# First attention pair: scores from split float32r operands of 64 rows, its rotation on VectorE, and zero matmuls ahead of the first data

## The chip, the cores and the metric

One core of a Trainium2 chip. Every time is in microseconds (us) on the device; a kernel's time is the median of its runs. The profile is one further execution, with its own time.

## The reference

Three stages in a row. Attention over 4 batches, 8 heads, 576 positions, head size 64; then two feed-forward blocks on the 2304 resulting rows of 512.

```python
q_rot, k_rot = rotate(q), rotate(k)          # rotary: x1*cos - x2*sin, x1*sin + x2*cos
scores = q_rot @ k_rot.T / sqrt(64)
attn = softmax(scores) @ v                   # -> x, 2304 x 512
h = x @ w_in;  x2 = (h - tanh(h)) @ w_out    # 512 -> 2048 -> 512
out = ((x2 @ w1) * (x2 @ w2)) @ w3 @ w_out2  # 512 -> 1024 -> 512
```

The change touches the attention alone, and there only what is done for the first of its 16 pairs of heads.

## The kernel before

**Pairs and steps.** Two heads of one batch are a pair, and lie on the partitions as 2 x 64 rows (head j in rows 64j to 64j+63). The 576 positions are 512 main ones and 64 tails. A pair has five steps (`steps`, L416): first c = NQ = 4, the tail queries of both heads in one block, then c = 0 to 3, 128 main queries for each head. I call them NQ and c0 to c3.

**One step.** `scores` (L298) writes one PSUM tile "sc" per head (two banks each; NQ has only one tile; there are two "sc" buffers in all), `exps` (L331) reads it on ScalarE, with the maximum that VectorE's reduction L327 found as bias. `norm` divides on GpSimd, `trans` (L359) transposes the result on TensorE three steps later (LAG_T), and `pv` multiplies by v from four steps later.

**The two ways of making scores.** From the second pair on, q and k are split in two float32r parts (hi and the rest), and `prep_q`, `prep_k` and `prep_t` (L219, L241, L264) move them by DMA into tiles of 128 rows (`qs`, `ks`), so that two matmuls of 128 rows and 288 columns give the three products. The first pair doesn't wait for such DMAs: `q_first`, `k_first` and `qt_first` are plain float32 tiles, and its scores are float32 matmuls whose operands are 64 rows of them (the trace shows two PE instructions for each). All four of head 0 come first, then the four of head 1.

**The rotation.** `rope` (L193) makes two products with the sine table on VectorE (L199), one product with the cosine table (L202) and a sum (L204). While `early[0]` is true, that is for the first pair and the first tails, L202 runs on GpSimd and L204 on VectorE.

**The order.** The program text is a list; a scheduler puts each engine's instructions in order, by place in the text and by what is ready in its own reckoning. On the chip each engine takes its list strictly in that order. The head (L467 to L481) is: DMAs for k, its table, tails, q, its table, the second pair, two weights; then rotation of k, `prep_k`, rotation of q and of the tails, `prep_t`, `prep_q`; then the loop over steps (L484), in which `prepare` (L446) makes the next pair ready in steps NQ, c0 and c1.

Of the kernel before, what the change touches and what calls it, by code (L numbers as in the profile page):

```python
# [42 lines left out]
def fused_kernel(tc, q, k, v, w_in, w_out, w1, w2, w3, w_o2, tables, out):  # L43
# [14 lines left out]
    def f32(ap):  # L58
        return ap.bitcast(F32)
# [133 lines left out]
    def rope(t, cos, sin, a):  # L193

        p, n, C = t.shape[0], t.shape[1], t.shape[2]
        a = a.rearrange("p c h d -> p h c d")
        hd = D // 2
        for o, i in ((0, hd), (hd, 0)):
            nc.vector.tensor_tensor(  # L199
                a[:, :, :, o:o + hd], t[:, :, :, i:i + hd],  # L200
                sin[:, :, o:o + hd].unsqueeze(1).to_broadcast([p, n, C, hd]), ALU.mult)
        (nc.gpsimd if early[0] or n > 2 else nc.vector).tensor_tensor(  # L202
            t, t, cos.unsqueeze(1).to_broadcast([p, n, C, D]), ALU.mult)
        (nc.vector if early[0] else nc.gpsimd).tensor_tensor(a, a, t, ALU.add)  # L204
# [12 lines left out]
    qk, first = {}, {}  # L217

    def prep_q(b, hp):  # L219
        a = rot["q", b, hp]  # L220
        ps = psum.tile([128, 512], F32, tag="t", name=f"tq_{b}_{hp}", bufs=4)
        for c in range(NQ):
            nc.tensor.transpose(ps[:, c * 128:(c + 1) * 128],
                                a[:, c, :, :].rearrange("p h d -> p (h d)"), ident)
        if (b, hp) == pairs[0]:
            t = att.tile([128, SM], F32, tag="qs0", name="q_first")
            nc.any.tensor_copy(t, ps)
            first["q"] = t
            return
        qp = slots.tile([128, 2, SM], F32R, tag="s15", name=f"qp_{b}_{hp}")  # L230
        nc.any.tensor_copy(qp[:, 0, :], ps)
        nc.vector.tensor_tensor(qp[:, 1, :], ps, f32(qp[:, 0, :]), ALU.subtract)
        qs = []
        for j in range(2):
            t = att.tile([128, SM], F32R, tag=f"qs{j}", name=f"qs{j}_{b}_{hp}")
            for r in range(2):
                nc.sync.dma_start(f32(t[64 * r:64 * r + 64]), f32(qp[64 * j:64 * j + 64, r, :]))
            qs.append(t)
        qk["q", b, hp] = qs

    def prep_k(b, hp):  # L241
# [9 lines left out]
        if (b, hp) == pairs[0]:  # L251
            t = att.tile([128, ST + S], F32, tag="ks0", name="k_first")
            nc.scalar.copy(t[:, ST:ST + SM], ps)
            first["k"] = t
            return
        kp = att.tile([128, 2, ST + S], F32R, tag="kp", name=f"kp_{b}_{hp}", bufs=1)
        m = slice(ST, ST + SM)
        nc.any.tensor_copy(kp[:, 0, m], ps)
        nc.vector.tensor_tensor(kp[:, 1, m], ps, f32(kp[:, 0, m]), ALU.subtract)
        qk["kp", b, hp] = kp  # L260
# [3 lines left out]
    def prep_t(b, hp):  # L264
# [5 lines left out]
        if (b, hp) == pairs[0]:  # L270
            t = att.tile([128, 128], F32, tag="qs1", name="qt_first")
            nc.gpsimd.memset(t, 0.0)
            first["t"] = t
            for j in range(2):
                p = slice(64 * j, 64 * j + 64)
                nc.vector.tensor_copy(t[p, p], ps[p, 0:64])
            for o in (0, ST + SM):
                nc.vector.tensor_copy(first["k"][:, o:o + 64], ps[:, 64:128])
            return
# [5 lines left out]
        ends = kp.rearrange("p t (n s) -> p t n s", s=ST)[:, :, ::S // ST, :]  # L285
        twice = ps[:, 64:128].unsqueeze(1).to_broadcast([128, 2, ST])
        nc.scalar.copy(ends[:, 0], twice)
        nc.vector.tensor_tensor(ends[:, 1], twice, f32(ends[:, 0]), ALU.subtract)
        for j, t in enumerate(qk["k", b, hp]):
            src = kp[64 * j:64 * j + 64, :, ST:] if j == 0 else kp[64:128, :, 0:S]  # L290
            for r in range(2):
                nc.sync.dma_start(f32(t[64 * r:64 * r + 64]), f32(src))
        qk["qt", b, hp] = qt
# [4 lines left out]
    def scores(i):  # L298
        b, hp, c = steps[i]
        e = att.tile([128, 2, S], F32, tag="e", name=f"e_{i}", bufs=E_BUFS)  # L300
        ss = []
        for j in range(2 if c < NQ else 1):
            s = psum.tile([128, 2, 512], F32, tag="sc", name=f"sc{j}_{i}", bufs=2)
            ss.append(s)
            for n in range(2):
# [3 lines left out]
                q_c = slice(c * 128, (c + 1) * 128)  # L309
                if (b, hp) == pairs[0]:  # L310
                    if c < NQ:
                        p = slice(64 * j, 64 * j + 64)
                        terms = [(first["q"][p, q_c], first["k"][p, keys if j else cols])]
                    else:
                        terms = [(first["t"], first["k"][:, cols])]
                elif c < NQ:
                    qs, ks = qk["q", b, hp], qk["k", b, hp]
                    terms = [(qs[j][:, q_c], ks[j][:, t, keys]) for t in range(2)]
                else:
                    qt, kp = qk["qt", b, hp], qk["kp", b, hp]  # L320
                    terms = [(qt[:, x, :], kp[:, y, cols]) for x, y in ((0, 0), (0, 1), (1, 0))]
                for t, (lhs, rhs) in enumerate(terms):
                    nc.tensor.matmul(s[:, n, 0:HS], lhs, rhs,  # L323
                                     start=t == 0, stop=t == len(terms) - 1)
# [141 lines left out]

    load_pair(*pairs[0], "k")  # L467
# [6 lines left out]
    next_load()  # L474
    rope_pair(*pairs[0], "k")
    prep_k(*pairs[0])
    rope_pair(*pairs[0], "q")
    rope_tail(0)
    prep_t(*pairs[0])
    prep_q(*pairs[0])  # L480
# [377 lines left out]
```

## Time and profile before

| what | us |
|---|---|
| median of 3 runs (lowest, highest) | 1120.63 (1110.46, 1121.62) |
| the profiled execution, its own time | 1120.93 |
| its span, first to last instruction | 1119.1 |
| first pair's scores, first matmul to the second pair's first | 13.5 to 42.1 |
| end of the last pair's exponentials | 321 |

The page gives each engine's busy time, the span in 40 slices, the DMA queues, and the chain that ended last, followed back from the end. A busy PE in it is an engine with a matmul in flight, at whatever clock. The rows on which the prediction rests stand in a section of their own below.

### The profile page before, as it was taken

Reading aid. Unit: us, or ns where it says so; the run is one execution under the profiler, and the core shown is the slowest. Engines: PE = TensorE matmul, PEld = TensorE weight load, DVE = VectorE, ACT = ScalarE, POOL = GpSimd, SP = SyncE. Lnnn points to the kernel's source line nnn. Section 1 sums busy time; section 2 is a strip of 40 time slices with the busy share of each in tenths; the row PEclk is TensorE's granted clock in tenths of the full one; section 3 lists DMA queues with packets and bytes.
Section 4 is the critical chain, followed back from the end, with each engine's and each line's share of the span. In section 5 each row is a group of like instructions: output and inputs, shape, how many; then the busy total and the mean of one; then the engine's idle time right before and its main releaser. Section 6 shows DMA issues by size and latency. Waiting matters only on the chain.

```text
span 1119.1 us, 15718 instructions
## 1 busy us (share of the span) xinstructions
PE 1066.4 (95%) x5598; PEld 856.6 (77%) x5598; DVE 783.2 (70%) x1439; ACT 563.0 (50%) x1195; POOL 394.1 (35%) x379
## 2 busy tenths in 40 slices
PE   6999899999998999999989899999899999999998
PEld 3676777777766788888767588898677888888887
DVE  5799999999959868669999978678985211212121
ACT  2577787777766555456656455555532111111121
POOL 3475686676472302024353320316531202002000
PEclk9999999999999999999999899999999999999999
DMA  5465667665612111012222111232531100101010
GB/s 178 122 174 139 176 157 203 158 173 127 167 38 76 38 57 57 29 36 87 76 73 97 57 48 50 92 114 95 205 124 47 38 1 1 38 1 38 1 38 20
DMA packets 64685, 96.37 MB, mean 86 GB/s; under 512 B 11616, under 2 KB 40288, under 8 KB 64608
## 3 DMA queue, kind: packets, MB, share of 16 engines
q1 hardware_dynamic: 64608, 95.38, 29.6%
q8 instruction: 44, 0.72, 0.3%
q14 instruction: 33, 0.27, 0.1%
HBM read 58.79 MB, written 11.01 MB: 62 GB/s over the span
## 4 chain that ended last, share of the span: by engine, by line
PE 66%; DVE 21%; issue 4%; ACT 4%; DMA 2%; POOL 1%; SPq 0%; DVEq 0%; ACTq 0%; POOLq 0%
PE pw L748 15%; PE x2p L581 11%; PE h L544 10%; PE o L771 8%; PE sc L323 7%; PE pv L408 4%; PE wp L628 4%; PE te L381 3%; DVE nm L327 2%; DVE g_q L562 2%; DVE g L567 2%; DVE g_s L561 1%; DVE g_q L564 1%; DVE g_t L563 1%; ACT e L334 1%
## 5 line engine op out<-in xcount | busy, mean ns | idle before, releaser
L581 PE MATMUL x2p<-g,s_out 128*128 128x512 f32 (+1 forms) x960 | 222.4, 378 | 22.3 <-DVE g L567 11.7
L581 PEld LDWEIGHTS x2p<-g,s_out 128*128 128x128 f32 x960 | 170.7, 193 | 63.1 <-DVE g L567 17.8
L345 POOL TENSOR_SCALAR e<-e,r 128x576 f32<-128x576 f32 x144 | 126.0, 887 | 81.7 <-DVE r L343 52.5
L754 DVE TENSOR_TENSOR ab<-a,pw 128x512 f32<-128x512 f32 (+1 forms) x40 | 25.3, 633 | 174.5 <-PE pw L748 173.9
L334 ACT ACTIVATE e<-sc,nm 128x576 f32<-128x576 f32 x144 | 107.8, 748 | 42.9 <-DVE nm L327 30.4
L327 DVE TENSOR_REDUCE nm<-sc 128x1 f32<-128x576 f32 x144 | 106.1, 747 | 21.4 <-PE sc L323 20.6
L771 PE MATMUL o<-wpt,abs 128*128 128x512 f32 x432 | 105.2, 390 | 0.7 <-DVE abs L757 0.5
L566 ACT CAST g<-g_q 128x512 fp32r<-128x512 f32 (+1 forms) x80 | 46.2, 578 | 106.8 <-DVE g_q L564 106.6
L771 PEld LDWEIGHTS o<-wpt,abs 128*128 128x128 f32 x432 | 80.3, 188 | 18.2 <-DVE abs L757 1.1
L323 PE MATMUL sc<-ks,qs 128*128 128x288 f32 x480 | 90.1, 318 | 3.5 <-ACT e L334 3.1
L323 PEld LDWEIGHTS sc<-ks,qs 128*128 128x128 f32 x480 | 67.9, 188 | 26.0 <-ACT e L334 11.5
L381 PE MATMUL te<-ident,e 128*128 128x128 f32 x576 | 84.9, 280 | 0.6 <-ACT eta L385 0.2
L561 DVE TENSOR_TENSOR g_s<-g_s,h 128x512 f32<-128x512 f32 (+1 forms) x80 | 50.4, 630 | 49.7 <-ACT g_m L560 49.4
L752 ACT COPY a<-pw 128x512 f32<-128x512 f32 (+1 forms) x40 | 21.7, 543 | 114.8 <-PE pw L748 114.8
L557 ACT ACTIVATE g_s<-h 128x512 f32<-128x512 f32 (+1 forms) x80 | 44.0, 550 | 61.2 <-PE h L544 59.8
L381 PEld LDWEIGHTS te<-ident,e 128*128 128x128 f32 x576 | 69.4, 145 | 6.3 <-issue 4.2
L567 DVE TENSOR_TENSOR g<-g_q,g 128x512 fp32r<-128x512 f32 (+1 forms) x80 | 59.0, 738 | 16.2 <-ACT g L566 15.4
L756 ACT CAST abs<-ab 128x512 fp32r<-128x512 f32 (+1 forms) x40 | 23.1, 576 | 84.3 <-DVE ab L754 84.3
L564 DVE COPY_PREDICATED g_q<-g_m,g_t 128x512 f32<-128x512 int32 (+1 forms) x80 | 62.9, 787 | 0.8
L562 DVE SCALAR_TENSOR_TENSOR g_q<-g_q,g_s 128x512 f32<-128x512 f32 (+1 forms) x80 | 61.5, 769 | 0.0
L558 ACT ACTIVATE g_q<-g_s,qb 128x512 f32<-128x512 f32 (+1 forms) x80 | 54.5, 681 | 2.6 <-DVE g L567 2.6
L560 ACT ACTIVATE g_m<-g_s,nt 128x512 f32<-128x512 f32 (+1 forms) x80 | 54.0, 676 | 0.0
(387 smaller groups left out, 2302.0 us busy)
## 6 DMA issues: line engine op xcount, KB each, us to landing
ks<-kp SPq DMA_DIRECT2D x60, 288.0 KB, 5.2
raw_w<-in_moe_w SPq DMA_DIRECT2D x32, 512.0 KB, 3.7
raw_in<-in_moe_w_in SPq DMA_DIRECT2D x16, 512.0 KB, 3.7
raw_out<-in_moe_w_out SPq DMA_DIRECT2D x16, 512.0 KB, 3.5
qs<-qp SPq DMA_DIRECT2D x60, 128.0 KB, 3.5
wp_dram<-wpe SPq DMA_DIRECT2D x24, 256.0 KB, 2.0
k<-in_k SPq DMA_DIRECT2D x16, 256.0 KB, 3.2
q<-in_q SPq DMA_DIRECT2D x16, 256.0 KB, 3.0
```

The source lines that it names most:

```text
L323: nc.tensor.matmul(s[:, n, 0:HS], lhs, rhs, start=t == 0, stop=t == len(terms) - 1)
L327: nc.vector.tensor_reduce(nm[:, j:j + 1], s[:, :, 0:HS], AX.XY, ALU.max, negate=True)
L334: nc.scalar.activation(d["e"][:, j, :].rearrange("p (n s) -> p n s", n=2), d["ss"][j][:, :, 0:HS], AF.Exp, bias=d["nm"][:, j:j + 1], accum ...
L345: nc.gpsimd.tensor_scalar(d["e"][:, j, :], d["e"][:, j, :], r[:, j:j + 1], 1.0, ALU.mult, ALU.mult)
L381: nc.tensor.transpose(ps[:, n * 128:(n + 1) * 128], e[:, o + n * 128:o + (n + 1) * 128], ident)
L544: nc.tensor.matmul(ps[:, 0:w], ws[:, a, kk], x[:, b_, 0:w], start=kc == 0 and t == 0, stop=kc == NK - 1 and t == 2)
L562: nc.vector.scalar_tensor_tensor(qq, qq, QC, s, ALU.add, ALU.mult)
L564: nc.vector.copy_predicated(qq, mk.bitcast(I32), t)
L567: nc.vector.tensor_tensor(g[:, 1, 0:w], qq, f32(g[:, 0, 0:w]), ALU.subtract)
L581: nc.tensor.matmul(x2ps[j][o][:, 0:w], ws[:, a, oo], g[:, b_, 0:w], start=c == 0 and t == 0, stop=c == HF - 1 and t == 2)
L748: nc.tensor.matmul(ps[:, 0:w], ws[:, a, kk], x[:, b_, 0:w], start=kc == 0 and t == 0, stop=kc == NK - 1 and t == 2)
L771: nc.tensor.matmul(outps[j][t], g[:, a, tt], wp[c][:, b_, :], start=c == 0 and i == 0, stop=c == NF2 - 1 and i == 2)
```

## The change

Four edits, all for the first pair:

1. `q_first`, `k_first`, `qt_first` go. `prep_q`, `prep_k` and `prep_t` split into float32r parts as for the other pairs, into slots that are not in use yet, and stop before the DMAs.
2. `scores` of the first pair takes three float32r products (hi by hi, hi by rest, rest by hi) straight from these 64-row tiles, and the matmuls of both heads alternate: head 0, head 1, head 0, and so on.
3. In `rope`, the cosine product of the first pair and the first tails moves from GpSimd to VectorE.
4. A tile of zeros is made, and 20 + 8 + 8 matmuls of 128 rows by 512 columns on it are put ahead of the rotation of k, ahead of that of q, and ahead of `prep_q`. Nothing reads their result.

```diff
-        (nc.gpsimd if early[0] or n > 2 else nc.vector).tensor_tensor(
+        (nc.gpsimd if n > 2 and not early[0] else nc.vector).tensor_tensor(
             t, t, cos.unsqueeze(1).to_broadcast([p, n, C, D]), ALU.mult)
...
+    TERMS = ((0, 0), (0, 1), (1, 0))
...
-        if (b, hp) == pairs[0]:
-            t = att.tile([128, SM], F32, tag="qs0", name="q_first")
-            nc.any.tensor_copy(t, ps)
-            first["q"] = t
-            return
-        qp = slots.tile([128, 2, SM], F32R, tag="s15", name=f"qp_{b}_{hp}")
+        first = (b, hp) == pairs[0]
+        qp = slots.tile([128, 2, SM], F32R, tag="s12" if first else "s15", name=f"qp_{b}_{hp}")
         nc.any.tensor_copy(qp[:, 0, :], ps)
         nc.vector.tensor_tensor(qp[:, 1, :], ps, f32(qp[:, 0, :]), ALU.subtract)
+        qk["qp", b, hp] = qp
+        if first:
+            return
...
         if (b, hp) == pairs[0]:
-            t = att.tile([128, ST + S], F32, tag="ks0", name="k_first")
-            nc.scalar.copy(t[:, ST:ST + SM], ps)
+            kp = [slots.tile([128, ST + S], F32R, tag=f"s{10 + t}", name=f"kp{t}_first")
+                  for t in range(2)]
...
+        nc.any.tensor_copy(kp[0][:, m], ps)
+        nc.vector.tensor_tensor(kp[1][:, m], ps, f32(kp[0][:, m]), ALU.subtract)
...
+                elif i < NQ + 1:
+                    p = slice(64 * j, 64 * j + 64)
+                    terms = [(qk["qp", b, hp][p, x, q_c], kp[y][p, keys if j else cols])
+                             for x, y in TERMS]
...
+                mms += [(n, t, j, t == len(terms) - 1, *ops) for t, ops in enumerate(terms)]
+        if i < NQ + 1:
+            mms.sort(key=lambda m: m[:3])
+        for n, t, j, last, lhs, rhs in mms:
+            nc.tensor.matmul(ss[j][:, n, 0:HS], lhs, rhs, start=t == 0, stop=last)
...
+    idle = slots.tile([128, SM], F32R, tag="s9", name="idle")
+    nc.gpsimd.memset(f32(idle), 0.0)
+    idle_ps = psum.tile([128, 512], F32, tag="t", name="idle_ps", bufs=4)
+
+    def spin(n):
+        for _ in range(n):
+            nc.tensor.matmul(idle_ps, idle[:, 0:128], idle, start=True, stop=True)
...
+    spin(20)
     rope_pair(*pairs[0], "k")
     prep_k(*pairs[0])
+    spin(8)
     rope_pair(*pairs[0], "q")
     rope_tail(0)
     prep_t(*pairs[0])
+    spin(8)
     prep_q(*pairs[0])
     early[0] = False
```

## Rows read from the trace of the kernel before

**Rows 1.** The page: busy time of two engines; the granted clock in 40 slices.
```profile
PE 1066.4 (95%) x5598; PEld 856.6 (77%) x5598; DVE 783.2 (70%) x1439; ACT 563.0 (50%) x1195; POOL 394.1 (35%) x379
PEclk9999999999999999999999899999999999999999
```
**Rows 2.** Windows: stretch, length, busy us of engines (instructions), granted clock, DMA share, GB/s.
```profile
13.50:42.10 28.60, 28.60 (x74) 16.93 (x73) 14.53 (x35) 12.88 (x32) 8.99 (x10) 1.00 0.53 139
44.70:321.00 276.30, 266.43 (x1888) 202.76 (x1886) 262.04 (x606) 207.13 (x534) 178.61 (x181) 1.00 0.62 158
339.30:341.70 2.40, 0.17 (x1) 0.00 (x0) 2.37 (x3) 0.85 (x2) 1.52 (x1) 1.00 0.48 191
341.70:345.10 3.40, 2.99 (x7) 2.41 (x8) 3.33 (x7) 2.65 (x5) 0.00 (x0) 0.50 0.00 0
400.00:420.00 20.00, 20.00 (x93) 16.54 (x92) 11.36 (x19) 10.32 (x18) 0.00 (x0) 1.00 0.20 68
```
**Rows 3.** The chain in order of time: start, us, what; first pair and after.
```profile
13.53 4.14 PE sc L323 x8
...
18.93 2.22 PE sc L323 x4
...
38.45 2.21 PE sc L323 x4
40.67 1.04 PE te L381 x4
...
42.14 1.44 PE sc L323 x6
43.58 1.40 PE te L381 x7
...
47.74 0.73 PE sc L323 x4
...
52.22 0.44 PE te L381 x4
...
57.05 1.87 PE pv L408 x14
...
61.60 0.88 PE sc L323 x6
```
**Rows 4.** Timeline of the head: start, us, engine, line, operation, [idle before].
```profile
0.94 0.31 POOL L184 MEMSET zero<- 128x256 f32 x1
4.59 0.76 DVE L199 TENSOR_TENSOR rak<-k,tab 128x256 f32<-128x256 f32 x2 [2.72 <-DMA tab<-tables]
5.43 1.26 POOL L202 TENSOR_TENSOR k<-k,tab 128x512 f32<-128x512 f32 x1 [3.71 <-DVE rak L199]
6.81 0.76 DVE L199 TENSOR_TENSOR rt<-tqk,tab 128x256 f32<-128x256 f32 x2 [1.46 <-DMA tqk<-in_k]
7.49 0.68 DVE L204 TENSOR_TENSOR rak<-rak,k 128x512 f32<-128x512 f32 x1
8.22 1.11 PE L248 MATMUL tk_first<-ident,rak 128*128 128x128 f32 x4 [8.22 <-DVE rak L204]
12.42 1.12 PE L223 MATMUL tq<-ident,raq 128*128 128x128 f32 x4 [1.37 <-DVE raq L204]
```
**Rows 5.** Timeline inside the first pair, from one score tile to its release.
```profile
17.60 1.11 PE L248 MATMUL tk<-ident,rak 128*128 128x128 f32 x4
19.68 0.69 DVE L259 TENSOR_TENSOR kp<-tk,kp 128x512 fp32r<-128x512 f32 x1 [0.19 <-ACT kp L258]
21.18 0.76 DVE L327 TENSOR_REDUCE nm<-sc 128x1 f32<-128x576 f32 x1 [0.81 <-PE sc L323]
21.97 0.74 ACT L334 ACTIVATE e<-sc,nm 128x576 f32<-128x576 f32 x1 [1.36 <-DVE nm L327]
22.61 0.19 ACT L334 ACTIVATION_READ_ACCUMULATOR e<-sc,nm 128x1 f32 x1
31.76 0.58 ACT L385 COPY eta<-te 128x512 f32<-128x512 f32 x1 [1.63 <-PE te L381]
```
**Rows 6.** Timeline: the second pair's DMA issues, and the first matmuls after a fall.
```profile
29.21 3.83 SPq L237 DMA_DIRECT2D qs<-qp  x4
342.11 2.07 PE L581 MATMUL x2p<-g,s_out 128*128 128x512 f32 x4 [2.65 <-ACT g L566]
343.99 0.63 PE L544 MATMUL h<-xs_(0, 0)_2_4331,s_in 128*128 128x512 f32 x1
```

More of the change, by code (lines that the diff above doesn't have):

```diff
@@ L214, in rope_tail @@
         rot["t", b] = a
-    qk, first = {}, {}
+    qk = {}
+    TERMS = ((0, 0), (0, 1), (1, 0))
     def prep_q(b, hp):
@@ L251, in prep_k @@
         if (b, hp) == pairs[0]:
-            t = att.tile([128, ST + S], F32, tag="ks0", name="k_first")
-            nc.scalar.copy(t[:, ST:ST + SM], ps)
-            first["k"] = t
-            return
[L256 to L260, printed above, removed]
+            kp = [slots.tile([128, ST + S], F32R, tag=f"s{10 + t}", name=f"kp{t}_first")
+                  for t in range(2)]
+        else:
+            kp = att.tile([128, 2, ST + S], F32R, tag="kp", name=f"kp_{b}_{hp}", bufs=1)
+            qk["kp2", b, hp] = kp
+            kp = [kp[:, t, :] for t in range(2)]
+        m = slice(ST, ST + SM)
+        nc.any.tensor_copy(kp[0][:, m], ps)
+        nc.vector.tensor_tensor(kp[1][:, m], ps, f32(kp[0][:, m]), ALU.subtract)
+        qk["kp", b, hp] = kp
+        if (b, hp) == pairs[0]:
+            return
         qk["k", b, hp] = [
@@ L269, in prep_t @@
             ident)
[L270 to L279, printed above, removed]
         kp = qk["kp", b, hp]
@@ L284, in prep_t @@
             nc.vector.tensor_tensor(qt[p, 1, p], ps[p, 0:64], f32(qt[p, 0, p]), ALU.subtract)
[L285 removed]
+        ends = [t.rearrange("p (n s) -> p n s", s=ST)[:, ::S // ST, :] for t in kp]
         twice = ps[:, 64:128].unsqueeze(1).to_broadcast([128, 2, ST])
[L287 to L288 removed]
+        nc.scalar.copy(ends[0], twice)
+        nc.vector.tensor_tensor(ends[1], twice, f32(ends[0]), ALU.subtract)
+        qk["qt", b, hp] = qt
+        if (b, hp) == pairs[0]:
+            return
+        both = qk["kp2", b, hp]
         for j, t in enumerate(qk["k", b, hp]):
[L290 removed]
+            src = both[64 * j:64 * j + 64, :, ST:] if j == 0 else both[64:128, :, 0:S]
             for r in range(2):
                 nc.sync.dma_start(f32(t[64 * r:64 * r + 64]), f32(src))
[L293 removed]
     HS = S // 2
@@ L300, in scores @@
         e = att.tile([128, 2, S], F32, tag="e", name=f"e_{i}", bufs=E_BUFS)
[L301 to L304, printed above, removed]
+        ss = [psum.tile([128, 2, 512], F32, tag="sc", name=f"sc{j}_{i}", bufs=2)
+              for j in range(2 if c < NQ else 1)]
+        kp, q_c = qk["kp", b, hp], slice(c * 128, (c + 1) * 128)
+        mms = []
+        for j in range(len(ss)):
             for n in range(2):
```

18 lines of the change are left out of this document (4 added, 14 removed).

## The prediction, made before the changed kernel was run

> **What bounds the kernel now.** I read the page first: TensorE is busy 95% of the span, VectorE 70%, so what TensorE does sooner should come out at the end [rows 1]. Then the stretches. While the first pair's scores run, 13.5 to 42.1 us, TensorE is busy for all of its 28.60 us with only 74 instructions, VectorE for half; from there to 321 us it does 1888 in 276.3 us, nearly seven a microsecond against 2.6, with VectorE at 262.04 us of it [rows 2]. So the first pair is bound by TensorE alone, and slowly; the fifteen pairs after it are bound by TensorE and VectorE together, at (321 - 42.1) / 15 = 18.6 us a pair. The first takes 28.6.
>
> Why so slowly, the chain tells. Four transposes cost 1.04 us at 40.67 and 0.44 at 52.22; six float32r matmuls of 288 columns cost 1.44 at 42.14 and 0.88 at 61.60 (0.24 and 0.147 each) [rows 3]. The same work takes 1.6 to 2.4 times as long, so I take it that TensorE ran on its lower level, 1.2 GHz, until the seven transposes of 43.58 ended (0.20 each). The clock column says 1.00 there [rows 2]; I trust the durations, and read that column as having no record yet. TensorE's work before 42 us had no rest but was nearly all float32 matmuls of 64 rows and transposes; the rise came behind the first float32r matmuls of 128 rows. Where the column does show a fall, it came after 2.40 us in which TensorE had one instruction [rows 2].
>
> **What the change removes, on TensorE.** In steps c0 to c3, from 13.53 + 4.14 - 2.21 = 15.46 to 42.14, that is 26.68 us, the chain holds eight score tiles at 2.21 each, 17.7 us (three of these pieces are in the rows; in the first, two NQ matmuls stand with the tile), and 9.0 us of transposes [rows 3]. A step is 6.67 us.
>
> **What it adds on TensorE.** Twelve float32r matmuls of 64 rows by 288 columns a step, which no row of before shows. Bounds, on the upper level: 12 at the 0.73 / 4 = 0.18 of the 128-row form give 2.2 us; six pairs at half of the low-clock 0.24 give 0.72. I take that the two heads overlap, as the v product does, whose matmuls take half the array's columns in alternation and come at 1.87 / 14 = 0.134, where full ones of that length would need twice as much by their columns [rows 3]: 12 x 0.09 = 1.1 us. On the lower level twice that, 2.2; without overlap 12 x 0.24 = 2.9. Three quarters of the score time go. The Trainium skill says as much: by "TensorE: Matmul & The Clock Gate" (What overlaps and what doesn't), matmuls in different row groups start some 4 ns apart; the sum by it would be the low end, 0.72 a step and 1.5 us less over the pair than mine. No run so far shows it for rows.
>
> **What is late next.** The alternation has a price. Before, head 0's tile needs only its own buffer, while the other is still read. Now the second matmul of a step belongs to head 1, so a step can't go on until both exponentials of the last have read their tiles. Step by step [rows 5]: scores end, reduction 21.18 to its exponential at 21.97, 0.83 with the hand-over; that exponential 0.64 to its accumulator read, 0.10 on to the next; a copy of a transposed tile between the two, 0.48 (31.76; without it 0); head 1's exponential 0.74; 0.05 to TensorE. Sum 2.84 us, without the copy 2.36. Head 1's reduction is done meanwhile. So a step is at least 1.1 + 2.84 = 3.9 us, whatever else TensorE does in between: its transposes, 9.0 / 4 / 2 = 1.1 us a step, fit into the wait. VectorE stands behind other pieces of up to 0.69 us when a tile comes; half a piece, 0.35, makes 4.3.
>
> The Trainium skill warns here: "Tiling speeds up TensorE but not PSUM evacuation" (TensorEngine Tiling (Array Packing), PSUM Bottleneck). This trace agrees, with 2.84 us of evacuation behind 1.1 us of matmul.
>
> TensorE now works only 1.1 + 1.1 of 4.3 us a step. That is above the stretch that preceded the fall (next to nothing in 2.40 us), below the 96% of the later pairs [rows 2], so I expect the clock to fall in part of the pair: two of the four steps with 2.2 in place of 1.1. The four steps: 4 x 4.3 + 2 x 1.1 = 19.4 us. Saved 26.7 - 19.4 = **7.3 us**. VectorE's 14.53 us of work in the old stretch, plus nothing new in c0 to c3, fit into 19.4; ScalarE's 12.88 too.
>
> **After the pair.** From 42.14 to about 44.7 the second pair ran on the lower level: 6 matmuls at 0.24 against 0.147 to 0.18, and five transposes at 0.20 against 0.11, **0.9 us** saved if the clock is up by then.
>
> **The head.** The cosine product of k took 1.26 us on GpSimd, and VectorE did the tails meanwhile; on VectorE it is one piece like L204's 0.68, so k's rotation ends at about 5.35 + 0.68 + 0.68 = 6.7 in place of 8.2 [rows 4]. VectorE has then three such products more (2.0 us) and the parts of k, q and the tails (two at 0.69, three small ones about 0.7), less the small copies that go; starting at 4.6 that ends near 12, and it had gaps of 1.46 us and more. But TensorE's list decides. The zeros are ready at about 0.94 + 0.31 + 0.62 (a memset twice as long) and a little, 2.3. A matmul of 512 columns costs (343.99 - 342.11) / 4 = 0.47 on the lower level [rows 6], 20 / 93 = 0.215 on the upper [rows 2]. If the clock rises half-way, at 7, ten cost 4.7 and ten 2.15: the first twenty end at 9.2, the k transposes come at 9.2 (before 8.22), 0.44 long, then eight zeros 1.7, the tail's transpose, eight zeros 1.7, q's transposes 0.44: 13.5, with VectorE done. q's parts need a copy 0.58 and a subtraction 0.69, so c0 starts at 14.9 with NQ's 1.1 us behind that cover. Against 15.46 that is **0.5 us** saved. If the list takes all 36 zeros first (the trace shows that it does move ready work forward: `tk` of the second pair runs at 17.60 between the score tiles of one step [rows 5]), they end at 12.5, q's transposes at 13.5, and c0 is the same within 0.7. Without a rise, see rival three. The head's bounds are +1.3 and -7.4.
>
> **DMAs.** None is added. The second pair's c0 needs `qs`, issued from 29.21 to 33.04 on SP's queue [rows 6]. It needed them at 47.7; now at about 15 + 19.4 + 4 = 38. Their issue moves forward with the splits of the second pair, so they cost nothing; if they don't move at all, there are still some 5 us less a landing of about 3.
>
> **Sum.** 7.3 + 0.9 + 0.5 = 8.7 us. The profiled execution took 1120.93, 1.8 us more than its span and 0.3 above the median, so 1120.9 - 8.7 = **1112 us**. All later stages should only move: after 42 us TensorE is at 96% and what feeds it has its place in the same lists. One of the three runs was 10 us below the others. No trace of it is here; a run in which the clock rose at the first scores would gain about as much, and then a part of this gain has already been in it.
>
> **Rivals.**
> *One, faster (chance 0.2):* the clock stays up and VectorE isn't in the way: 4 x 3.9 = 15.6, saved 11.1 + 0.9 + 0.5, **1108.5**; with the low end of the matmuls 1107. For it: VectorE has half its time free in this stretch. Against: TensorE idles half of it.
> *Two, the matmuls don't overlap or the clock is down for the whole pair (0.2):* 2.2 to 2.9 us a step, the middle 2.6 + 2.84 + 0.35 = 5.8, four 23.2, saved 3.5, nothing behind it, head 0.5: **1117**. For it: 64-row matmuls never raised the clock before. Against: the column halves overlap.
> *Three, slower (0.1):* multiplying zeros doesn't raise the clock, and all 36 stand ahead of the k transposes: 36 x 0.47 + 2.3 = 19.2; then transposes 0.8, k's parts 1.4, NQ 1.44, so c0 starts at 22.9, 7.4 us late, and the slow steps of rival two give back only 3.5: **1125**. It decides as soon as the zeros end more than 7 us after the k rotation is ready. For it: nothing in this trace shows what zeros do to the clock. Against: instructions of that form hold the upper level for whole stages [rows 2].
> *My forecast* has 0.5, and its own range is 1109 to 1115.
>
> **The numbers.** Rivals one to two span 1107 to 1117, three adds 1125; leaving out half of three and the edge of one, the range is 1106.5 to 1119.5. A measurement here can tell about 1% from no change, that is below 1109.4 or above 1131.8. Below: most of rival one (0.17) and a part of my case (0.14), 0.31. Above: the far end of three, 0.04. Within: 0.65.
>
> **What would show it.** Zeros on TensorE from about 2.3 us, their spacing going from 0.47 to 0.215 before 10; first `tk` transposes at 8.5 to 10 and 0.44 long; c0's scores at about 15; twelve matmuls in 1.1 (to 2.2); each step's scores waiting on ScalarE's second exponential, steps of 4 to 5 us; the second pair's first scores near 34 in place of 42.1; the attention's end near 312. It is wrong if the second pair starts as early as that but the end of the attention doesn't move (VectorE would then be the bound), or if the zeros keep their 0.47 spacing.

## The result, and the profile after

The changed kernel took **1124.3 us** (median of 20 runs, 1122.01 to 1128.36). The kernel before, run beside it 20 times, took 1120.6 (1109.81 to 1124.20). The ratio on record, which is taken over all runs and is not that of the medians (1.0033), is 1.0075 with an interval of 1.0049 to 1.0100: slightly slower, where 1112 was forecast. The profiled execution took 1127.65 (two of the 20 runs took longer) with a span of 1125.8; one further execution that was profiled later took 1121.18. Two single runs took over twice as long as all others, 3628.57 (br_pin) and 2644.13 (before, beside b_mask and nm_pin), and are left out of the medians, ranges and ratios below.

The median of before hides two groups: 9 of its 20 runs lay between 1109.8 and 1111.9, the other 11 between 1120.6 and 1124.2, and nothing between. The trace of [rows 1] is of the upper group. The changed kernel has one group only.

The page of after: busy time of the engines, then the granted clock in 40 slices. The first slice has the clock at 0.6, where [rows 1] has a 9.

```profile
PE 1070.5 (95%) x5652; PEld 867.3 (77%) x5652; DVE 789.2 (70%) x1445; ACT 563.6 (50%) x1196; POOL 385.9 (34%) x376
PEclk9699999998999999999999999999999999999999
```

Windows of after (columns as in [rows 2]). The second row answers to the first there; its clock is 0.66. The third is the stretch between the fall of the clock and its next rise: TensorE busy for nearly all of it, at the lower level (0.50), with 92 instructions in 23.89 us.

```profile
8.20:13.50 5.30, 5.30 (x16) 4.13 (x15) 3.85 (x8) 1.20 (x2) 0.00 (x0) 1.00 0.79 272
13.50:42.10 28.60, 27.22 (x113) 21.31 (x112) 19.67 (x42) 13.38 (x35) 8.91 (x9) 0.66 0.54 136
22.69:46.58 23.89, 23.75 (x92) 19.80 (x92) 14.33 (x36) 13.00 (x33) 7.75 (x10) 0.50 0.40 90
44.70:321.00 276.30, 262.13 (x1850) 201.52 (x1849) 256.51 (x597) 202.74 (x522) 170.27 (x177) 0.98 0.62 156
```

Timeline of after, TensorE (answers to [rows 4, 5]): the head, one step of the first pair, the hand-over to the second pair, and a stall much later.

```profile
6.95 0.66 PE L249 MATMUL tk_first<-ident,rak 128*128 128x128 f32 x2 [6.95 <-DVE rak L204]
7.26 7.23 PE L471 MATMUL idle_ps<-idle 128*128 128x512 f32 x20
14.33 0.38 PE L249 MATMUL tk_first<-ident,rak 128*128 128x128 f32 x2
14.47 2.09 PE L471 MATMUL idle_ps<-idle 128*128 128x512 f32 x8
...
18.36 0.60 PE L225 MATMUL tq<-ident,raq 128*128 128x128 f32 x4
...
21.94 0.53 PE L321 MATMUL sc<-kp_first,qtd 128*128 128x288 f32 x2 [0.85 <-DVE kp_first L282]
...
22.73 4.85 PE L321 MATMUL sc<-kp_first,qp 64*128 64x288 f32 x16
...
31.74 1.80 PE L321 MATMUL sc<-kp_first,qp 64*128 64x288 f32 x6
33.47 1.11 PE L378 MATMUL te<-ident,e 128*128 128x128 f32 x4
34.52 1.81 PE L321 MATMUL sc<-kp_first,qp 64*128 64x288 f32 x6
...
43.00 1.79 PE L321 MATMUL sc<-kp,qtd 128*128 128x288 f32 x6
...
240.25 0.80 PE L321 MATMUL sc<-ks,qs 128*128 128x288 f32 x4 [1.57 <-ACT e L331]
```

The scheduler put the first 20 zeros *between* the second and the third of the four k transposes. They waited for k until 6.95, as the transposes before them did, and then held up the rest of k until 14.33. They did raise the clock, at 12.45 (their spacing goes from 0.43 to 0.23). VectorE's timeline shows what the late k let in:

```profile
12.43 0.43 DVE L115 TENSOR_SCALAR z_in<-z_in 128x512 f32<-128x512 f32 x1 [1.13 <-ACT z_in L113]
...
15.43 0.68 DVE L261 TENSOR_TENSOR kp_first<-tk_first,kp_first 128x512 fp32r<-128x512 f32 x1
...
17.36 1.65 DVE L120 SCALAR_TENSOR_TENSOR z_in<-raw_in,z_in 128x512 int32<-128x512 int32 x1
...
19.77 1.79 DVE L118 SCALAR_TENSOR_TENSOR z_out<-raw_out,z_out 128x512 int32<-128x512 int32 x1
21.59 0.29 DVE L282 TENSOR_TENSOR kp_first<-tt,kp_first 128x128 fp32r<-128x128 f32 x1
```

Conversions of weights (`z_in`, `z_out`) that the kernel needs hundreds of microseconds later stand ahead of k's last part (21.59), for which TensorE waits 0.85 us before 21.94.

Where the 6.7 us between the two profiled executions lie (times of before from [rows 3] and its timeline):

| from, to | before | after | change |
|---|---|---|---|
| start to c0's scores | 15.46 | 22.73 | +7.3 |
| c0's scores to the second pair's first scores | 26.68 | 20.27 | -6.4 |
| these to the second pair's first exponential (45.5; 45.7) | 3.4 | 2.7 | -0.7 |
| that to the end of the last pair's exponentials (320.9; 327.2) | 275.4 | 281.5 | +6.1 |
| that to the end of the span | 798.2 | 798.6 | +0.4 |

(Two of c0's twelve matmuls had gone ahead at 20.56; the table counts from the other ten, at 22.73.) So the pair's saving came, the head ate it, and the fifteen pairs behind it, which were only to move, lost six more. In the later execution of after that stretch was 277.7, +2.3.

### The profile page after: what moved, and what is told of

Read it like the earlier page. It is cut to its first block, busy times and chain, and to the rows that moved or that the text cites. A ratio compares the mean times of both kernels' runs of the same rounds, so it can differ in the third digit from the quotient of the medians.

```text
span 1125.8 us, 15823 instructions
## 1 busy us (share of the span) xinstructions
PE 1070.5 (95%) x5652; PEld 867.3 (77%) x5652; DVE 789.2 (70%) x1445; ACT 563.6 (50%) x1196; POOL 385.9 (34%) x376
## 4 chain that ended last, share of the span: by engine, by line
PE 60%; DVE 26%; ACT 5%; issue 5%; DMA 2%; POOL 2%; DVEq 0%; SPq 0%; ACTq 0%; POOLq 0%
PE pw L757 15%; PE x2p L590 9%; PE h L553 8%; PE o L780 8%; PE sc L321 6%; PE pv L405 4%; PE wp L637 3%; PE te L378 3%; DVE nm L324 3%; DVE g_q L571 2%; DVE g L576 2%; DVE g_q L573 2%; DVE g_s L570 2%; DVE g_t L572 2%; ACT e L331 2%
## 5 line engine op out<-in xcount | busy, mean ns | idle before, releaser
L342 POOL TENSOR_SCALAR e<-e,r 128x576 f32<-128x576 f32 x144 | 120.5, 849 | 85.9 <-DVE r L340 48.6
L324 DVE TENSOR_REDUCE nm<-sc 128x1 f32<-128x576 f32 x144 | 106.5, 749 | 19.9 <-PE sc L321 18.7
L780 PEld LDWEIGHTS o<-wpt,abs 128*128 128x128 f32 x432 | 80.4, 188 | 17.8 <-DVE abs L766 1.0
L573 DVE COPY_PREDICATED g_q<-g_m,g_t 128x512 f32<-128x512 int32 (+1 forms) x80 | 65.4, 818 | 0.8
```

The costliest lines, as they stand in the source:

```text
L324: nc.vector.tensor_reduce(nm[:, j:j + 1], s[:, :, 0:HS], AX.XY, ALU.max, negate=True)
L342: nc.gpsimd.tensor_scalar(d["e"][:, j, :], d["e"][:, j, :], r[:, j:j + 1], 1.0, ALU.mult, ALU.mult)
L573: nc.vector.copy_predicated(qq, mk.bitcast(I32), t)
L780: nc.tensor.matmul(outps[j][t], g[:, a, tt], wp[c][:, b_, :], start=c == 0 and i == 0, stop=c == NF2 - 1 and i == 2)
```

## The experiments

Medians (of ten runs, b_mask of four, n_pin2 of twelve, nm_pin2 of eleven, br_pin of nine), each with the ratio to the kernel before on the same chip; the first two rows are single executions. "Body" is the stretch of 275.4 above, from the second pair's first exponential to the end of the last; the times in the last three columns are of the one execution that was profiled.

| kernel | us (lowest, highest) | ratio, interval | clock up, down, up | second pair's first exponential | body |
|---|---|---|---|---|---|
| before (again, three executions) | 1123.2; 1121.16; 1110.87 | | 45.6; 45.4; 16.3 | 45.5; 46.3; 33.3 | 276.8; 275.5; 276.3 |
| after (again) | 1121.18 | | 10.2, 23.8, 44.3 | 44.7 | 277.7 |
| nospin | 1117.78 (1116.14, 1119.71) | 1.0015 [0.9981, 1.0050] | 35.75 | 41.9 | 275.9 |
| dvezero | 1121.88 (1120.27, 1123.62) | 1.0056 [1.0019, 1.0093] | 7.55, 17.79, 41.7 | 40.7 | 281.2 |
| b_spin | 1124.02 (1122.45, 1125.93) | 1.0080 [1.0042, 1.0118] | 8.4, 18.6, 49.3 | 47.3 | 278.0 |
| alt | 1122.7 (1121.99, 1124.23) | 1.0076 [1.0042, 1.0110] | 40.7 | 42.9 | 279.2 |
| dvz_alt | 1122.88 (1121.31, 1125.83) | 1.0064 [1.0030, 1.0097] | 7.56, 17.80, 41.7 | 42.8 | 280.7 |
| rot | 1122.41 (1121.05, 1127.07) | 1.0062 [1.0027, 1.0097] | 15.0, 18.45, 42.3 | 42.1 | 278.1 |
| b_pin | 1124.3 (1113.39, 1128.73) | 1.0073 [1.0026, 1.0120] | 44.5 | 46.0 | 281.0 |
| br_pin | 1115.15 (1113.34, 1122.88) | 1.0008 [0.9965, 1.0052] | 10.35, 17.2, 41.1 | 41.1 | 281.0 |
| n_pin | 1116.46 (1113.57, 1118.36) | 1.0015 [0.9974, 1.0055] | 12.9, 16.3, 33.4 | 39.8 | 275.2 |
| n_mask | 1112.15 (1110.52, 1114.12) | 0.9950 [0.9917, 0.9983] | 22.65 | 35.9 | 276.5 |
| b_mask | 1117.89 (1116.36, 1120.47) | 1.0075 [1.0055, 1.0096] | 16.3 | 33.4 | 281.2 |
| nm_pin | 1110.44 (1108.27, 1113.44) | 0.9971 [0.9937, 1.0006] | 10.3 | 33.4 | 276.3 |
| n_pin2 | 1117.29 (1114.39, 1119.94) | 1.0013 [0.9979, 1.0047] | 10.9, 17.7, 34.8 | 39.2 | 274.9 |
| nm_pin2 | 1111.20 (1108.82, 1112.66) | 0.9954 [0.9922, 0.9987] | 15.4 | 34.1 | 276.2 |

The ratios hang on how the runs of before split into their two groups beside each kernel; medians in microseconds compare better between rows, to some 1.5 us, by which the middle of each group of before differs between the chips.

**1. The place of the zeros.** *nospin* is after without its zero matmuls (nothing reads their result). *dvezero* changes one word of after. *b_spin* is before with the zeros alone.

```diff
-        for _ in range(n):
+        for _ in range(0):
```

```diff
-    nc.gpsimd.memset(f32(idle), 0.0)
+    nc.vector.memset(f32(idle), 0.0)
```

> The changed kernel without its 36 zero matmuls, all else as it is. Theory A (place of the zeros): twenty of them stand between the k transposes and hold up the head; without them the k transposes run at once at about 7 us, c0's scores start near 15 to 16 in place of 24, and the first pair, at the low clock as before, takes the same 19 us, so the second pair starts near 35 to 37 and the kernel takes about 1124 - 7 = 1117 us. Theory B (the clock decides, not the place): without zeros the clock is low from the start, as it was low in the changed kernel from 22.7 us; the first pair gains nothing and the kernel stays at 1124 or slower. Theory C (the loss is in the later pairs, where the profile of the changed kernel lost 6 us between 235 and 275 us at falls of the clock): the second pair starts 7 us earlier but the end stays near 1124.

> The changed kernel with one word changed: VectorE writes the zeros, not GpSimd. The list of TensorE then begins with 25 zero matmuls, ahead of the k transposes, and VectorE's list has no weight conversions in the head. Theory A: zeros run from about 2 us, the clock rises before 9, k transposes end near 10, c0's scores start near 16, clock up for at least part of the pair; second pair near 34 to 36, kernel 1110 to 1117 us. Theory B: clock falls as before when VectorE is waited for, and the kernel stays at 1120 to 1124. Theory C: second pair early, end near 1124.

> The kernel before with the 36 zero matmuls alone (float32 scores, rotation on GpSimd). TensorE's list begins with twenty zeros ahead of the k transposes. Theory A: the zeros end at about 9 to 10, head a little late (1 to 3 us), the clock is up when the scores begin; if it stays up, a float32 score tile costs 1.1 in place of 2.2 us and the kernel takes the time of the lower group of the runs of before, 1110. Theory B: the 64-row scores let the clock fall again, 1121 to 1124 us.

Without the zeros the time falls by 6.5 us: the first exponential is at 20.6 (after: 23.3), the second pair's 3.8 us earlier than in after, and the body is 275.9. So the zeros as placed, together with the lists that came with them, cost about that much: 2.7 us are there at the first exponential, 3.8 at the second pair's, the rest in the body. With *dvezero* the list changes: 25 zeros run ahead of any k data, no conversion gets into VectorE's head. Timeline of dvezero, TensorE:

```profile
1.45 8.81 PE L471 MATMUL idle_ps<-idle 128*128 128x512 f32 x25 [1.45 <-DVE idle L466]
10.10 0.60 PE L249 MATMUL tk_first<-ident,rak 128*128 128x128 f32 x4
...
17.65 0.27 PE L271 MATMUL tt<-ident,rt 128*128 128x128 f32 x1
19.22 1.81 PE L321 MATMUL sc<-kp_first,qp 64*128 64x288 f32 x6 [1.30 <-ACT e L331]
```

The clock is up at 7.55, down at 17.79 (six matmuls 1.81 again), and up at 41.7. The second pair comes 5 us earlier than in after, but the body is 281.2 and the time only 2.4 us below after. *b_spin* shows the same on the kernel before: raised at 8.4, lost at 18.6, time 1124. Of the 48 score matmuls of c0 to c3 the raised clock reached six in dvezero; in b_spin it fell 0.1 us after the first had begun (18.48).

**2. The order of the heads.** In after the alternation of the text is gone from the list: six of head 0, then six of head 1. *alt* (no zeros) and *dvz_alt* (dvezero) force it with edges that only fix the order.

```diff
-            nc.tensor.matmul(ss[j][:, n, 0:HS], lhs, rhs, start=t == 0, stop=last)
+            m = nc.tensor.matmul(ss[j][:, n, 0:HS], lhs, rhs, start=t == 0, stop=last)
+            if prev is not None and 0 < i < NQ + 1:
+                tc.add_manual_dep(m.ins, prev.ins.name, mybir.DependencyInfo(
+                    mybir.DependencyClass.NoSync, mybir.DependencyReason.DATA), reason="order")
+            prev = m
```

> The changed kernel without zeros, with the first pair's score matmuls of c0 to c3 held to the alternating order of the text by order-only edges (in the changed kernel the scheduler put head 0's six first, then head 1's six, at 0.29 us each). If matmuls of the two row halves overlap as the forecast took, twelve cost 1.5 to 2.2 us at the low clock (0.12 to 0.18 each) in place of 3.5; if they don't, they stay at 0.24 to 0.29 each, 2.9 to 3.5. Either way a step then waits for head 1's exponential: with overlap a step is 2 + 2.84 + the rest, near 5, about what it is now, and the kernel stays within 2 us of the 1117.8 without the order; without overlap a step is 6.5 and the kernel is 4 to 7 us slower than that.

> The same order in the kernel whose zeros VectorE writes (zeros first, clock up from 7.5 us). If the matmuls overlap and the clock stays up for part of the pair, twelve cost 0.7 to 1.1 us there and the step is bound by reduction and exponentials, 3.9 to 4.3, kernel 1112 to 1118 us. If TensorE, being then idle for half of a step, loses the clock as it did at 17.8 us, the pair runs at the low clock and the kernel stays at 1120 to 1124.

Timeline of alt, TensorE, three steps of the first pair:

```profile
18.63 1.80 PE L322 MATMUL sc<-kp_first,qp 64*128 64x288 f32 x11 [1.50 <-ACT e L336]
...
23.53 2.53 PE L322 MATMUL sc<-kp_first,qp 64*128 64x288 f32 x12 [0.79 <-ACT e L336]
26.05 1.97 PE L383 MATMUL te<-ident,e 128*128 128x128 f32 x8
27.81 0.42 PE L393 MATMUL te<-ident,e 128*128 128x128 f32 x1
28.58 2.53 PE L322 MATMUL sc<-kp_first,qp 64*128 64x288 f32 x12 [0.34 <-ACT e L336]
```

In the first row the alternating matmuls of a step (eleven of the twelve have a record) take 1.80 us, as long as six of one head do in after (1.74 to 1.81). So the two row halves overlap in full. The single records show it too: the starts lie in pairs, at most 7 ns apart, one pair each 0.24 us, and one head alone starts one matmul each 0.24 us behind its first. In the later steps twelve take 2.53 us, because the second matmul, head 1's first, starts 0.72 us behind the first (24.25 behind 23.53): the exponential that still reads head 1's buffer ends at 24.20. So the forecast's price is paid twice, ahead of a step's scores (0.34 to 0.79, in the first row 1.50) and inside them.

Both kernels are no faster than with the heads apart. From its own first exponential to the second pair's, the first pair takes 25.2 us in alt and 21.4 in nospin, 25.5 in dvz_alt and 22.4 in dvezero; the second pair comes 1 and 2 us later, since the forced kernels have an earlier head. The median of alt is 4.9 us above that of nospin, which its expectation had given to matmuls that do not overlap; most of it lies in the body (279.2 against 275.9).

**3. The rotation alone, and a few pinned zeros.** *rot* is before with the cosine products on VectorE. *b_pin* is before with 6 zeros pinned in the gaps of TensorE behind the k and the tail transposes, *br_pin* both together; *n_pin* is after with 8 zeros pinned (2, 4, 2) in place of 36. In all three VectorE writes the zeros.

```diff
+            tc.keep_in_program_order(
+                nc.tensor.matmul(idle_ps, idle[:, 0:128], idle, start=True, stop=True))
```

> The kernel before with the cosine products of the first pair on VectorE and nothing else. If the rotation is what the changed kernel without zeros gains over the upper group of before (1117.8 against 1121), this takes 1118 in its upper group and 1107 to 1109 in its lower; if it gains nothing, its groups are those of before, 1110 and 1121, and the three products make the difference.

> The kernel before with six zero matmuls and nothing else of the change: three pinned behind the k transposes, three behind the tail's transpose, in gaps of 1.3 and 1.4 us in which TensorE waits anyway (written by VectorE). Theory (what matters is that TensorE has no pause between its first transposes and the first scores, and that nothing stands ahead of them): the clock is up by about 16 us in every run, scores 1.16 us a tile, second pair's first exponential near 33 to 35, and all runs lie at 1109 to 1113 us, the lower group of before. Rival (zeros as such do harm, or the first pair falls back to the low clock): 1117 to 1124, or two groups as before.

> As the kernel before with six pinned zeros, and the cosine products of the first pair on VectorE besides. If the rotation on VectorE brings the k transposes 1.4 us earlier and q's part is not later, the kernel is up to 1.5 us faster than the one with pinned zeros alone; if VectorE's added work stands ahead of q's sum, the same or 1 us slower. A pause that opens between the transposes may let the clock rise later: then two groups.

> The changed kernel with eight zero matmuls in place of 36: two behind the k transposes, four behind the tail's, two behind q's, each pinned in a gap. Theory: head as without zeros (c0 near 15 to 16), clock up by 16 and held through the first pair because TensorE has work in its list for nearly all of it; kernel 1106 to 1113. Rival: the three-product scores leave pauses (two exponentials, splits) and the clock falls as at 22.7 us in the changed kernel; kernel 1116 to 1120, as without zeros.

The rotation brings the first exponential 1.5 us forward (14.8 against 16.3) and the second pair 3.4, but the body gives 2.7 back, and none of its ten runs is in before's lower group, where two groups, at 1118 and at 1107 to 1109, were expected. b_pin's zeros were a miss: in its profiled execution they did not raise the clock in the head at all, 3 of its 10 runs lay at 1113 to 1115, the rest above 1123. br_pin and n_pin raise it, and lose it at 17.2 and 16.3. n_pin is 8 us better than after: its eight zeros fit into gaps, and its first exponential (18.4) is no later than without any (nospin 20.6). Against nospin it gains 1.3, which is within the difference between chips.

**4. What the two groups of before are.** Further executions of before and after with nothing changed.

> The kernel before, unchanged, for a second profile. Its 20 runs lie in two groups, 1110 to 1112 and 1120 to 1124 us. If the groups differ by when the clock rises in the first pair, a run of the lower group shows four transposes at 0.44 us well before 44 us; a run of the upper group shows 1.04 until then.

> The kernel before once more, for a profile of a run of its lower group (1108 to 1111 us). Theory: in such a run the clock rises during the first pair, well before 44.7 us; the second pair's first exponential then comes near 35 in place of 45.5. Rival: the first pair is the same and the 10 us lie in another stage.

> As the run before it: the kernel before, for a profile of its lower group. Theory: clock up during the first pair, second pair's first exponential near 35 us. Rival: the 10 us lie elsewhere.

> The changed kernel once more, for a second profile. Theory: the head repeats (twenty zeros between the k transposes, c0 near 24 us, clock falling at about 22 and rising near 46); the falls at 241 and 261 us need not repeat, and the time is 1122 to 1128. Rival: the falls between 235 and 275 us come every time and are the larger part of the loss.

The third of before fell into the lower group. Timeline of that execution of before, TensorE:

```profile
15.18 1.77 PE L323 MATMUL sc<-k_first,q_first 64*128 64x288 f32 x4
...
17.57 1.23 PE L323 MATMUL sc<-k_first,q_first 64*128 64x288 f32 x4
...
21.33 1.23 PE L323 MATMUL sc<-k_first,q_first 64*128 64x288 f32 x4
```

The clock rises at 16.29, within the first score tile, and stays. A tile costs 1.23 (1.16 in the chain) where [rows 3] has 2.21; the second pair's first exponential is at 33.3 in place of 45.5, and the time is 10 us lower. The upper group waits for the rise until 44.7 to 45.6, behind the second pair's first matmuls of 128 rows. From 17.5 to 31 TensorE is busy for 12.84 of 13.50 us in the one, all of 13.50 in the other; each keeps its level.

**5. The rows of the scores.** *n_mask* (nospin) and *nm_pin* (n_pin) take the first pair's scores over all 128 rows: q's parts are copied into one tile for each head whose other 64 rows are zeros. Matmuls, columns and result stay; q's copy and subtraction are made for each head by itself. *b_mask* does that to the float32 scores of before. *n_pin2* and *nm_pin2* run the twins with pinned zeros on one chip.

```diff
-                    p = slice(64 * j, 64 * j + 64)
-                    terms = [(qk["qp", b, hp][p, x, q_c], kp[y][p, keys if j else cols])
+                    terms = [(qk["qp", b, hp][j][:, x, q_c], kp[y][:, keys if j else cols])
...
+    qz = [slots.tile([128, 2, SM], F32R, tag=t, name=f"qz{j}") for j, t in enumerate(("s9", "s12"))]
+    for j in range(2):
+        nc.gpsimd.memset(f32(qz[j][64 - 64 * j:128 - 64 * j]), 0.0)
```

> The changed kernel without zero matmuls, and with the first pair's score matmuls on 128 rows: for each head a q tile whose other 64 rows are zero, so the products are the same, the number of matmuls too, in the same order of the lists. Theory (the clock stays low through the first pair because its scores use 64 rows): the clock rises within the first steps, by about 24 us in place of 35.8, twelve matmuls cost 1.5 to 2.2 us in place of 3.5, the second pair's first exponential comes near 35 to 38 in place of 41.9, kernel 1109 to 1114 us in one group. Rival (the clock stays low because of the pauses and the transposes between): the rise stays near 36 us, kernel 1116 to 1119.

> The masked 128-row float32r scores of the kernel that took 1112.15, and eight zero matmuls pinned in the gaps of the head (2 behind the k transposes, 4 behind the tail's, 2 ahead of q's). Theory (with 128-row scores a clock that the zeros raise is held): up at 11 to 13, no fall in the first pair, second pair's first exponential near 34 to 35 against 35.9 without zeros, time 1110 to 1112. Rival (the zeros only take the place of what TensorE waits for, and the raised clock falls in a wait of the head): a fall near 16 to 18 and a second rise some 4 us later, second pair at 36 or later, 1112 to 1115.

> The changed kernel with eight pinned zeros, again, beside its twin with masked 128-row scores on the same chip. Theory (64-row scores can't hold the clock that the zeros raise): 1116.5 as before, clock up at about 13, down again at about 16, up near 33. Rival (the difference between the two lay between chips): equal to its twin within 2 us.

> Eight pinned zeros and masked 128-row scores, again, on the same chip as the twin with 64 rows. Theory (128-row scores hold the clock): 1110.4, no fall in the first pair, 6 us below the twin. Rival (the difference lay between chips): equal to the twin within 2 us.

> The kernel before, with the first pair's float32 scores taken on 128 rows: q is copied into two tiles, one for each head, whose other 64 rows are zeros; count, columns and order of the matmuls stay. Theory (the 64-row form of the scores is what keeps TensorE at its lower level through the first pair): the clock rises within the first pair, some microseconds behind the first c0 scores, in every run; a float32 score tile then costs 1.16 us in place of 2.21, the second pair's first exponential comes near 36 in place of 45.5, and the runs form one group near 1111 to 1114. Rival (what kept it low in the kernel before is float32 itself, or the transposes, not the rows): the clock comes up at 44 to 46 as before, and the time is 1121 with two groups as before.

Without zeros the clock rises at 22.65 with 128 rows, at 35.75 with 64. Windows ahead of the rise, of nospin and then of n_mask (the clock column reads 1.00, as there is no record yet; the durations say otherwise):

```profile
18.00:35.70 17.70, 16.51 (x62) 13.00 (x63) 9.70 (x23) 7.91 (x22) 4.94 (x6) 1.00 0.46 104
```

```profile
16.00:22.60 6.60, 5.31 (x24) 4.87 (x23) 4.09 (x10) 2.87 (x8) 2.02 (x2) 1.00 0.43 118
```

In the first TensorE is busy for 16.51 of 17.70 us and the clock does not rise; in the second it rises after a stretch with less work in it, 5.31 of 6.60 us. In nospin it rose at 35.75, at the end of twelve transposes with no score between them (33.52 to 36.05). The twins with pinned zeros say the same of holding it. Window of n_pin2, then of nm_pin2, the first pair:

```profile
17.00:34.00 17.00, 15.70 (x63) 12.58 (x63) 10.27 (x27) 8.96 (x25) 4.94 (x6) 0.52 0.55 123
```

```profile
17.00:34.00 17.00, 12.57 (x91) 10.65 (x90) 15.66 (x37) 12.39 (x32) 10.23 (x10) 1.00 0.73 173
```

And their timelines, TensorE, n_pin2 first:

```profile
17.14 0.27 PE L271 MATMUL tt<-ident,rt 128*128 128x128 f32 x1
18.71 1.80 PE L321 MATMUL sc<-kp_first,qp 64*128 64x288 f32 x6 [1.30 <-ACT e L331]
20.44 1.11 PE L225 MATMUL tq<-ident,raq 128*128 128x128 f32 x4
```

```profile
16.89 0.27 PE L279 MATMUL tt<-ident,rt 128*128 128x128 f32 x1
18.56 1.05 PE L328 MATMUL sc<-kp_first,qz 128*128 128x288 f32 x6 [1.40 <-ACT e L338]
19.73 0.66 PE L225 MATMUL tq<-ident,raq 128*128 128x128 f32 x4
```

Both have the same wait for the first exponential, 1.30 and 1.40 us, at the same place. The 64-row twin loses the clock at 17.7 and has it back at 34.8; the 128-row twin, *less* busy (12.6 us of 17 against 15.7, in part because its matmuls run faster), keeps it. Six matmuls cost 1.05 instead of 1.80. The times are 1117.29 and 1111.20, and their ranges don't touch. The fall in n_pin2, at 17.72, comes 0.3 us into its wait; nm_pin2 keeps its clock through all 1.40 us, and so does nm_pin, whose clock had risen at 10.3, nearly when that of n_pin2 did (10.9). So the wait alone is not what costs the clock: it is lost, and stays down for 17 us, where the work around the wait is 64-row float32r matmuls. The masked kernel with few zeros is the best one here: 13 us below after, and all its runs lie about where before's lower group lies.

The mask on before shows less. The clock is up at 16.29 in the profiled execution, but so it is in before's lower group without a mask. The second pair starts 12 us earlier than in the upper group, and yet the time is 1117.89, since the body is 281.2. Timeline of b_mask, TensorE:

```profile
17.47 1.24 PE L324 MATMUL sc<-k_first,qz 128*128 128x288 f32 x4
...
150.36 0.48 PE L268 MATMUL tt<-ident,rt 128*128 128x128 f32 x1 [3.15 <-POOL rt L204]
```

**6. The body.** Times from one pair's first exponential to the next's, seventh to ninth and eleventh to thirteenth pair:

| kernel | 7th | 8th | 9th | 11th | 12th | 13th | body |
|---|---|---|---|---|---|---|---|
| before; its lower group | 18.4; 18.4 | 17.6; 17.6 | 18.1; 18.1 | 18.1; 18.2 | 19.9; 19.9 | 18.8; 18.8 | 275.4; 276.3 |
| after; again | 18.4; 18.4 | 20.9; 20.9 | 18.1; 18.1 | 16.8; 16.8 | 20.7; 20.7 | 23.5; 20.5 | 281.5; 277.7 |
| b_mask | 18.8 | 24.7 | 18.3 | 19.1 | 18.5 | 17.8 | 281.2 |
| br_pin | 18.4 | 23.6 | 18.3 | 19.1 | 18.5 | 17.8 | 281.0 |
| alt | 16.3 | 25.2 | 18.5 | 19.1 | 18.5 | 17.8 | 279.2 |
| nospin | 18.4 | 18.6 | 18.3 | 18.6 | 17.7 | 18.8 | 275.9 |
| n_mask; nm_pin2 | 18.4; 18.9 | 18.7; 18.0 | 18.2; 18.3 | 18.6; 18.6 | 17.7; 17.7 | 18.8; 18.8 | 276.5; 276.2 |

In these pairs the pattern belongs to the kernel, not to the execution: before has the same lengths to a tenth with either clock, the two executions of after agree except in the thirteenth pair, and three kernels from different parents share nearly one pattern with an eighth pair of 23.6 to 25.2. In b_mask TensorE waits 3.15 us for the tails' rotation, which GpSimd's list has behind three pieces of `norm` (row at 150.36). None of these lines is in the diffs; what differs is the place that the scheduler gave them. I made no run that changes this order and nothing else, so the cause is read from the traces and not shown by an edit. In after the extra stalls are in the 8th, 12th and 13th pairs; the one at 240.25 (1.57 us for an exponential) stands beside a fall of the clock at 241.1, which the second execution has at 238.9. Another fall, from 261.6 to 268.5, is in the first execution alone; it lies in the thirteenth pair, which is 3.0 us longer there.

## Why the prediction was wrong, by its own steps

*What bounds the kernel, and the clock read from durations* held: the first pair was TensorE alone at its lower level, and the lower group of before, 10 us down as the prediction suspected of the one low run, is the same kernel with the clock up at 16.3.

*The head, "0.5 us saved", c0 at 14.9*, is the step that failed first: c0's main block came at 22.73, 7.3 us late. Each part of the sum was near. K's rotation ended at 6.8 (forecast 6.7), the zeros were ready at 2.3 (2.3), they cost 0.43 and then 0.23 (0.47 and 0.215), and the clock rose. What failed is the order: I weighed zeros ahead of k and all 36 ahead of it, and both let TensorE multiply while it waits. The list has them behind k's first transposes, so that they begin when the data is there. The chain of after has the price in one row, and the pair's first scores in another:

```profile
7.61 6.88 PE idle_ps L471 x20
...
24.20 3.38 PE sc L321 x12
```

My bounds for the head, +1.3 and -7.4, held the value at their end, but I had tied that end to zeros that don't raise the clock, with 0.1. Rival three gave 1125 with c0 at 22.9; both came, by a mechanism that was not its own, which is luck.

The zeros are not all of the head's delay. At head 1's matmuls of c0, which all three kernels start in one piece, before is at 18.93, nospin at 21.46 (its first rotation waited 1 us longer for the table, to 5.54 in place of 4.59) and after at 24.20. So 1.5 to 2.5 us are there without zeros: the list mixes NQ's six products with head 0's six of c0 (14.28 to 19.4 in nospin), and TensorE then waits 1.19 us for NQ's exponential, where the forecast had NQ cover q's split. Taking the zeros out gave back 6.5 us (nospin), pinning eight of them in gaps 7.8 (n_pin).

*"The clock to fall in part of the pair: two of the four steps"* was wrong in size and in reason. I tied it to TensorE's waits. It was down from c0's third matmul to the end of c3, although TensorE had next to no waits there (busy for 23.75 of 23.89 us), and the twins, which differ in the rows of the scores, part on just this. Before the run I had written down the row for this, that 64-row work did not raise the clock in 27 us without rest, and gave it to rival two; it deserved the main place.

*The two heads overlap, 1.1 us a step on the upper level and 2.2 on the lower*: the mechanism was right and the order was not there. The alternation did not survive the scheduler: in after no two score matmuls of the pair start within 0.2 us of each other, and a step's cost 3.5 us. Where the order is forced, and nothing is waited for inside, a step's take 1.80 on the lower level (alt). The Trainium skill's "TensorE: Matmul & The Clock Gate" (Why this matters for your kernels) has matmuls in different row groups run at the same time, started at most 4 ns apart; the trace of alt agrees, but for starts of up to 7 ns. The row of the v product that I leaned on was no proof, though. Its matmuls have 256 columns,

```profile
56.98 1.94 PE L408 MATMUL pv<-etb,v 128*64 128x256 f32 x14
```

and at 0.215 for 512 [rows 2] that is 0.11 each without any overlap, against the 0.134 that I read as half price.

*"What is late next"*, a step bound by the exponentials at 4.3 us: in after no step waits for one, TensorE bounds it, at 20.27 / 4 = 5.1 us, which is some 3.3 of score matmuls (46 of the 48 lie in this stretch) and 1.8 of transposes. That the sum of c0 to c3 came within 1 us of the forecast (20.3 against 19.4) is chance. In the forced order the wait is there, as the prediction had it; that "this trace agrees", with 1.1 us of matmul, was said of a trace that has no such matmuls, and alt's rows are the first to show it.

*After the pair, 0.9 us*: not there, the six matmuls at 43.00 took 1.79, as long as before's (41.79), and the clock rose at 46.58. The 0.7 us of the table come from elsewhere: in before a copy of 0.59 us (45.00) stands on ScalarE ahead of that exponential.

*"All later stages should only move"* failed for the attention: +6.1 us in one execution, +2.3 in the other. The prediction named this sign (an early second pair and an unmoved end) but put it down to VectorE as a bound. Windows of the body, before and then after:

```profile
45.50:320.90 275.40, 265.53 (x1882) 202.19 (x1881) 261.18 (x603) 206.53 (x534) 178.16 (x181) 1.00 0.62 159
45.70:327.20 281.50, 267.24 (x1890) 205.22 (x1889) 259.83 (x604) 205.95 (x530) 173.22 (x181) 0.98 0.61 155
```

VectorE is busy for 259.83 us of after's body, no more than in before (261.18); the added time is in stalls and in falls of the clock, and that both come with another list is read from the traces. Behind the attention nothing changed (798.2 and 798.6).

The median adds one thing that no step had: the change takes away the lower group, nearly half of before's runs. Against the upper group alone after is some 3 us slower.

## What to carry to other kernels

A filler instruction is only a filler if the order holds it in a gap: its operands being ready early says nothing, so pin it, or give it a size that costs nothing where it lands. Before an operation is swapped for one with fewer rows, ask which level of the clock it will run at; padding 64 rows with zeros to 128 cost nothing in matmul time here (six took 1.81 us on the lower level in n_mask, 1.80 with 64 rows in n_pin2) and gave 6 us. It gives up the overlap of the two halves; what that would be worth on the upper level, no run here shows. And where a scheduler makes the lists, an edit at the start reshuffles what comes later: price it with some microseconds of either sign, and compare a milestone behind the edit with the end.

## What the runs showed of the hardware

Matmuls on zeros raise the clock as others do: up at 7.55 in dvezero, with nothing but zeros on TensorE until then. With 64-row float32r scores and transposes the granted clock stayed at 0.50 over 23.89 us in which TensorE was busy for 23.75 (after), while the same number of 128-row matmuls, half of whose operand rows are zeros, brought it up at 22.65 (n_mask) and held it with TensorE busy for 12.57 of 17.00 us (nm_pin2). The Trainium skill's "TensorE: Matmul & The Clock Gate" (Part 1, What's actually happening) has the level follow how busy the engine has been; by the busy column of these rows that is not all there is to it. 64-row float32 matmuls fit neither side fully: before stays down with them in one execution; in another the clock rose at 16.29, 1.1 us after they had begun, and stayed; in br_pin it was up from 10.35, they began at 13.07, and it fell at 17.18. Why rows count is not settled here. Matmuls on the two row halves, alternating, start in pairs at most 7 ns apart, a pair each 0.24 us on the lower level, where one half alone starts one each 0.24 us (alt, after).
